# Windowed attention and a routed expert: the prologue rebuilt (batch 0's q and k in the weight buffers, V behind them, masks added by TensorE, pooling by tile, casts on three engines)

## The chip, the cores and the metric

One core of one Trainium2 chip. The time is device microseconds of one execution; the lower the better. "The kernel before" is the kernel as it was, "the changed kernel" the one with the change. A ratio is the mean time of one kernel's fast runs over that of the kernel before's fast runs of the same rounds, so it is not quite the ratio of the medians that are quoted. A run counts as slow when it is more than 1.5% above the fastest of the same kernel.

## The reference

```python
B, H, S, D = 8, 8, 576, 64          # attention, float32
scores = q @ k.T / 8
scores = where(abs(i - j) <= 32, scores, -1e9)
x = softmax(scores) @ v             # -> (8, 576, 512)
logits = x.mean(axis=1) @ w_gate    # one row a batch, 8 experts
e = argmax(logits)                  # one expert a batch
out = p[e] * (relu(x @ w1[e]) @ w2[e])     # w1 512x1024, w2 1024x512
```

What matters here: a batch's expert is known only after the attention of all its 576 rows, and only then can its two megabytes of weights be asked for. For seven of the eight batches another batch's work covers that. For the first there is nothing before it: that is the prologue. In what follows, the pooled sums are these column means, a bank is one of TensorE's output buffers, the mask is the window of the second line, and a semaphore is a counter by which a transfer tells that it has landed.

## The kernel before

A planner in the file orders operations by priority and by its own estimate of times, and emits them engine by engine. Batch 0's loads, all on SyncE's queue, V in two parts between q and k:

```python
buffers("raw", [P, 2, J, D], FP32, 5)          # q or k of half a batch
...
def load(op, b=b, quad=quad, name=name, src=src):
    t = op.got["raw"][0]
    nc.sync.dma_start(t..., src[b, 4 * quad : 4 * quad + 4]...)
plan.add("SP", 0.6, f"ld{name}{b}{quad}", load, takes=[("raw", 1)], land=650e3, prio=base + quad)
...
def msk(op, half=half, quad=quad):             # VectorE, every batch
    nc.vector.tensor_tensor(ev, ev, mv, ALU.mult)
...
def pool(op):                                  # 20 matmuls behind the last normalisation
    for dt in range(NDT):
        for i in range(NQT):
            nc.tensor.matmul(bank[:, dt : dt + 1], xs_of[(b, i)]..., onec, ...)
```

Each output tile is evacuated by ScalarE and its store issued by ScalarE at once:

```python
def evac(op, i=i):
    nc.scalar.activation(osb[:, 0:w], bank_of.pop(f"2{b}{i}")[:, 0:w], ACTF.Copy, ...)
...
def store(op, i=i):
    nc.scalar.dma_start(out[b, 128 * i : 128 * i + 128, :], osb)
```

The softmax here doesn't subtract the row's maximum and nothing guards it: scores larger than these inputs give would overflow.

## Time and profile before

| | kernel before |
|---|---|
| time | 241.48 us (241.28 to 241.85, 3 runs) |
| expert of batch 0 known | 29.68 us |
| its weights asked for | 32.70 us |
| first expert matmul | 42.20 us |
| pooled sums copied, batches 0 to 7 | 27.87, 51.29, 79.64, 105.20, 130.73, 156.27, 181.80, 207.35 us |

The last row is the clock of the whole kernel: from batch 2 to batch 7 one batch every 25.5 us. A shift that is made or lost anywhere shows as a shift of all later entries, and the interval in which it happened is the one that is not 25.5. The busy time by stretches shows the one place after the prologue where TensorE is not full (columns: stretch, then busy us of TensorE, its weight loads, VectorE, ScalarE and GpSimd, then granted clock, DMA share, GB/s):

```profile
60.00:80.00 20.00, 17.59 (x211) 14.23 (x209) 10.50 (x31) 10.46 (x23) 3.39 (x6) 0.91 1.02 303
```

and the waits of that stretch (us in total, times, longest) say that it is one wait of ScalarE:

```profile
ACT hT L775 <- issue: 4.5, 1, 4.5
...
PE bank L757 <- ACT hT L775: 2.4, 1, 2.4
```

"issue" there is the store that the prediction speaks of: ScalarE's queue stood at issuing it.

### The profile page before, as it was taken

The numbers are of one execution on the slowest core, as the hardware profiler recorded it, in microseconds if no ns is written. First come the engines' busy times: TensorE is split into PE (matmuls) and PEld (weight loads), VectorE is DVE, ScalarE is ACT, GpSimd is POOL, SyncE is SP. The second block draws the span as 40 slices with busy tenths as digits, with TensorE's granted clock in tenths as the row PEclk, the third lists the DMA queues.
The fourth block names the chain that finished last, engine by engine and source line by source line (L and its number), as shares of the span: only waits on it lengthen the run. The fifth ranks groups of instructions, "written<-read, shape, count | busy, mean of one in ns | idle before, by whom it ended". The sixth has DMA issues, their size and how long they took to land.

```text
span 240.9 us, 6498 instructions
## 1 busy us (share of the span) xinstructions
PE 222.2 (92%) x2602; PEld 178.4 (74%) x2602; DVE 152.4 (63%) x390; ACT 172.6 (72%) x345; POOL 88.3 (37%) x134
## 2 busy tenths in 40 slices
PE   7999897999969989998999899989999899999980
PEld 6887685997558956996599758975799569848740
DVE  7999869765743796668865896589667746300000
ACT  8698783669626796779767994799487967637640
POOL 7652583059022494019701890069203300110000
PEclk9999999999997999999999999999999999999996
DMA  6978999999999999989999999979912992099431
GB/s 232 270 211 253 327 298 226 260 386 208 244 328 325 322 242 210 339 275 290 195 325 312 268 213 288 300 191 216 251 33 24 190 229 106 3 166 228 154 135 61
DMA packets 30014, 55.02 MB, mean 228 GB/s; under 512 B 6560, under 2 KB 15648, under 8 KB 27936
## 3 DMA queue, kind: packets, MB, share of 16 engines
q0 software_dynamic: 2304, 16.78, 36.9%
q1 hardware_dynamic: 22032, 28.39, 35.7%
q10 hardware_dynamic: 5648, 9.44, 10.6%
q8 instruction: 20, 0.33, 0.5%
q14 instruction: 10, 0.08, 0.1%
HBM read 61.94 MB, written 9.44 MB: 296 GB/s over the span
## 4 chain that ended last, share of the span: by engine, by line
PE 57%; DMA 18%; ACT 8%; SPq 6%; DVE 5%; issue 2%; POOL 1%; ACTq 1%; POOLq 0%
PE bank L757 21%; PE bank L793 17%; DMA raw<-in_q_dram 8%; DMA w<-in_moe_w_dram 7%; PE bank L601 6%; ACT qT L372 5%; PE bank L639 3%; PE bank L522 3%; DMA raw<-in_k_dram 3%; DVE qT L370 2%; SPq L427 2%; PE bank L799 2%; ACT kT L372 2%; SPq L383 2%; PE bank L667 2%
## 5 line engine op out<-in xcount | busy, mean ns | idle before, releaser
L757 PE MATMUL bank<-xT,w 128*128 128x288 f16 x512 | 77.5, 291 | 3.9 <-ACT hT L775 2.4
L400 POOL CAST qkb<-raw 128x640 bf16<-128x640 f32 x64 | 52.5, 853 | 75.5 <-issue 36.7
L775 ACT ACTIVATE hT<-bank 128x288 f16<-128x288 f32 x128 | 52.0, 415 | 26.7 <-PE bank L757 15.1
L757 PEld LDWEIGHTS <-w 128*128 128x128 f16 x512 | 60.4, 146 | 4.8 <-issue 2.5
L793 PE MATMUL bank<-w,hT 128*128 128x512 f16 x256 | 60.5, 379 | 0.0
L819 ACT ACTIVATE osb<-bank,gwb 128x512 f32<-128x512 f32 (+1 forms) x40 | 26.3, 658 | 22.3 <-PE bank L793 18.0
L793 PEld LDWEIGHTS <-hT 128*128 128x128 f16 x256 | 23.8, 98 | 22.8
L554 ACT ACTIVATE E<-bank 128x512 f16<-128x512 f32 x72 | 40.4, 626 | 0.3 <-PE bank L522 0.3
L571 DVE TENSOR_TENSOR E<-E,mask 128x1024 f16<-128x1024 f16 (+1 forms) x40 | 31.1, 818 | 6.3 <-ACT E L554 6.0
L601 PEld LDWEIGHTS <-E 128*128 128x128 f16 x576 | 26.3, 99 | 5.8 <-issue 0.8
L601 PE MATMUL bank<-vaug,E 128*128 128x65 f16 x576 | 29.1, 195 | 0.6 <-DVE vaug L455 0.4
L522 PE MATMUL bank<-qT,kT 128*128 128x128 bf16 x288 | 24.5, 219 | 4.7 <-ACT qT L372 4.0
L522 PEld LDWEIGHTS <-kT 128*128 128x128 bf16 x288 | 19.9, 97 | 11.8 <-issue 5.2
L625 DVE TENSOR_TENSOR xs<-bank,linv 128x256 f16<-128x256 f32 x64 | 27.2, 425 | 2.2
L370 DVE COPY qT<-bank 64x640 bf16<-64x640 bf16 (+1 forms) x32 | 24.5, 772 | 5.5 <-ACT qT L372 3.0
L343 PE MATMUL bank<-wide,zero 128*128 128x256 f16 x170 | 26.0, 285 | 1.4 <-POOL wide L268 1.4
L623 DVE RECIPROCAL linv<-bank 128x4 f32<-128x4 f32 (+1 forms) x80 | 14.1, 176 | 20.7 <-PE bank L601 20.7
L372 ACT COPY qT<-bank 64x512 bf16<-64x512 bf16 (+1 forms) x32 | 23.5, 741 | 3.3 <-DVE qT L370 1.8
L475 PE MATMUL bank<-id_bf,qkb 128*128 128x128 bf16 x288 | 22.5, 219 | 1.5 <-POOL qkb L400 1.0
L440 POOL CAST vaug<-vraw 128x576 f16<-128x576 f32 (+1 forms) x32 | 22.5, 788 | 1.4 <-DMA vraw<-in_v_dram 1.4
L727 POOL DMA_DIRECT2D w<-in_moe_w_dram x8 | 4.7, 587 | 44.9 <-DVE gw L719 21.2
L475 PEld LDWEIGHTS <-qkb 128*128 128x128 bf16 x288 | 18.1, 98 | 2.8 <-POOL qkb L400 1.4
(63 smaller groups left out, 199.4 us busy)
## 6 DMA issues: line engine op xcount, KB each, us to landing
w<-in_moe_w_dram POOLq DMA_DIRECT2D x16, 1024.0 KB, 11.9
raw<-in_q_dram SPq DMA_DIRECT2D x16, 576.0 KB, 6.9
raw<-in_k_dram SPq DMA_DIRECT2D x16, 576.0 KB, 6.4
out_dram<-osb ACTq DMA_DIRECT2D x32, 256.0 KB, 5.8
out_dram<-osb ACTq DMA_DIRECT2D x8, 128.0 KB
vraw<-in_v_dram SPq DMA_DIRECT2D x1, 576.0 KB
vraw<-in_v_dram SPq DMA_DIRECT2D x1, 544.0 KB, 5.8
vraw<-in_v_dram SPq DMA_DIRECT2D x8, 8.0 KB
```

The source lines that it names most:

```text
L370: nc.vector.tensor_copy(dst, src)
L372: nc.scalar.copy(dst, src)
L400: nc.gpsimd.tensor_copy(dst, src)
L475: nc.tensor.transpose(pv[:, j - j0, :], qkb_of[(b, quad, name)][:, j], id_bf)
L522: nc.tensor.matmul(dst, qkT[(b, a, "k")][:, k0 : k0 + P], qkT[(b, a, "q")][:, :, k0 : k0 + 64], start=(m == 0), stop=True, skip_group_chec ...
L554: nc.scalar.activation(dst, src, ACTF.Exp, bias=0.0, scale=0.125)
L571: nc.vector.tensor_tensor(ev, ev, mv, ALU.mult)
L601: nc.tensor.matmul(bank[:, hp * 65 : hp * 65 + 65], E_of[b][:, h, c0 : c0 + P], va_of[b][:, late, slot, 0:65], start=(hp == 0 and n == 0), ...
L625: nc.vector.tensor_tensor(xv[:, quad], hv[:, :, 0:64], linv.to_broadcast([n, 4, 64]), ALU.mult)
L757: nc.tensor.matmul(bank[:, 0:288], w_of[b][0].rearrange("p t (c n) -> p t n c", c=P)[:, dt, ft], xT_of[b][:, dt, 288 * c : 288 * c + 288], ...
L775: nc.scalar.activation(h_of[(b, ft)][:, 288 * c : 288 * c + 288], bank_of.pop(gn)[:, 0:288], ACTF.Relu,)
L793: nc.tensor.matmul(bank, h_of[(b, ft)][:, 128 * i : 128 * i + 128], w2s[:, ft, :], start=(ft == 0), stop=(ft == NFT - 1),)
```

## The change

The intent: know batch 0's expert earlier, ask for its weights earlier, and so start the steady stage earlier. Its core, cut:

```diff
+    roomy = [t.rearrange(...).bitcast(FP32)... for t in (w1s[0], w2s[0], w1s[1], w2s[1])]
...
-                    t = op.got["raw"][0]
+                    t = op.got["raw"][0] if b else roomy.pop(0)
-                    nc.sync.dma_start(
+                    (nc.scalar if op.eng == "ACT" else nc.sync).dma_start(
...
+                other = b == 1 and quad == 0        # batch 1's first q, k: issued by ScalarE
+                plan.add("ACT" if other else "SP", 0.6, f"ld{name}{b}{quad}", load,
...
-                    plan.add("SW/ACT" if b == 1 else "SW",
+                    plan.add("ACT" if b == 0 and part else "SW/ACT" if b < 2 else "SW",
...
+                if b < EARLY:                       # EARLY = 2
+                    ... bias of 0 or -16384, one matmul a bank, before the scores
+                    nc.tensor.matmul(out, id_bf, bv, start=True, stop=True, skip_group_check=True)
...
-            if pp == 0 and half < 2:
+            if pp == 0 and half < 2 or b < EARLY:   # no mask on VectorE
                 continue
...
-        def pool(op):
+        for i in range(NQT):
+            def pool(op, i=i):                      # four matmuls a tile, as tiles come
```

V of batch 0 comes in one large transfer behind q and k; small constants move from VectorE to GpSimd. The diff also makes GpSimd's casts of batch 2 wait until batch 1's weights are asked for (a dependency named `W10_`), splits the matmul banks into two pools and changes the planner's own model of loads.

## The prediction

> **What bounds the kernel now.** I read the page first, then busy time by stretches, the chain of waits, and the timeline of the first 45 us.
>
> ```profile
> span 240.9 us, 6498 instructions
> PE 222.2 (92%) x2602; PEld 178.4 (74%) x2602; DVE 152.4 (63%) x390; ACT 172.6 (72%) x345; POOL 88.3 (37%) x134
> ...
> PEclk9999999999997999999999999999999999999996
> DMA  6978999999999999989999999979912992099431
> ```
>
> TensorE is the bound, but its 222 us are not all work. The row of the line that only multiplies zeros[...]:
>
> ```profile
> L343 PE MATMUL bank<-wide,zero x170: 271/273/418, 1.4 to 40.2; 128*128 128x256 f16 x170
> ```
>
> It runs until 40.2 us, so the kernel has a prologue of about 42 us (batch 0's attention, its routing, the load of the expert's first weights) and then a stage in which TensorE never runs dry:
>
> ```profile
> 40.00:50.00 10.00, 8.61 (x121) 8.09 (x120) 7.58 (x25) 5.16 (x13) 0.96 (x2) 1.00 1.02 282
> ...
> 80.00:100.00 20.00, 19.23 (x221) 14.56 (x219) 16.26 (x35) 16.19 (x32) 11.53 (x15) 1.00 1.01 269
> 100.00:120.00 20.00, 19.22 (x221) 14.97 (x220) 15.52 (x34) 16.97 (x35) 11.53 (x15) 1.00 0.98 264
> ```
>
> First column after the stretch is TensorE: 96% busy. The pooling matmuls recur at 78.96, 104.53, 130.06, 155.59 and 181.14 us, 25.5 us a batch. So a prologue shorter by x ends the kernel x earlier, if nothing gives it back before this pace sets in. The chain of waits shows what stands in that gap:
>
> ```profile
> 32.70 9.45 DMA w<-in_moe_w_dram
> ...
> 42.20 0.71 PE bank L757 x4
> ...
> 55.17 14.94 DMA raw<-in_q_dram
> 70.19 1.12 ACTq L832
> 71.36 0.42 ACT hT L775
> 71.82 1.18 PE bank L757 x8
> ```
>
> Batch 0's weights are asked for at 32.70, land at 42.15, and the first expert matmul follows. Later a q load of batch 3, issued at 55.17, lands at 70.11, and only then does ScalarE issue a store of batch 0 whose data was ready at 66.88 (its evacuation started at 66.41 and took 0.47): ScalarE stands for 4.5 us and TensorE for 2.4. The built program says why: the transfers of SP and ACT take eight completion semaphores in turn, and each waits for the one that used its semaphore before. The store shared one with that load.
>
> The prologue itself:
>
> ```profile
> 2.85 5.68 SPq L427 DMA_DIRECT2D vraw<-in_v_dram  x1
> ...
> 19.06 1.92 DVE L571 TENSOR_TENSOR E<-E,mask 128x1024 f16<-128x1024 f16 x3
> ...
> 26.40 0.42 DVE L625 TENSOR_TENSOR xl<-bank,linv 64x256 f16<-64x256 f32 x1
> ...
> 29.41 1.28 POOL L400 CAST qkb<-raw 128x640 bf16<-128x640 f32 x2 [0.15 <-POOL qkb L400]
> 29.53 0.15 DVE L701 FIND_INDEX8 idx<-top,lg 1x8 uint32<-1x8 f32 x1
> ...
> 32.70 0.69 POOL L727 DMA_DIRECT2D w<-in_moe_w_dram  x1 [0.37 <-issue]
> ```
>
> SP stands 5.7 us behind the first big V load, so the second k is issued at 8.58 and lands at 12.9; VectorE's last three mask multiplications (1.92 us from 19.06) run right up to its first normalisation at 20.91; the last normalisation ends at 26.8, the expert is known at 29.68, and GpSimd, still casting, asks for the weights 3.0 us later.
>
> [...] the q load above took 14.94 us beside two weight loads, against a median of 6.9. [...] In 56.0 to 62.8 us the weights (queue q0, big packets) starve the SP queue (q1):
>
> ```profile
> q0 software_dynamic: 157, 1.16, 84.0%
> q1 hardware_dynamic: 147, 0.22, 10.1%
> ```
>
> [...] here eight 512-column matmuls take 1.73 us in the chain, 216 each. [...] here the page's clock dips to 7 tenths just after the 2.4 us stall, with 288-column matmuls of up to 448 instead of 286 ns.
>
> **The change, part by part.** Batch 0's four q, k loads go into the idle weight buffers, back to back, V behind them. From the rates in the trace (first bytes at 2.2 us, some 0.38 MB/us for 2304-byte pieces) 2.36 MB land by about 8.5, so the second k comes 4.4 us earlier. V then shares the engines with batch 1's first q, k, now issued from ACT near 9.5; I expect it at 14 to 16, against 14.9: no gain, but none is needed.
>
> Masks: five VectorE multiplications leave batch 0 (0.69, 0.91 and 1.92 us) and five batch 1; TensorE gets 9 bias matmuls a batch, 9 x 0.216 = 1.9 us, in time that was filled with zeros (the order of the built program has 113 of those matmuls in place of 170). This costs nothing on the path.
>
> Casts: part goes to ScalarE, so in the new order VectorE makes eleven of batch 0's twelve transposed copies alone. It starts them at 7.75 (7.37 when its constants end before, plus an estimated 0.35 for the bias). Five of 0.72 to 0.83 for the first half, six more, 8.7 us in all with little waiting: 16.4. So the scores of the second half start at 16.6, as before (16.84). What shrinks comes after: four exponentials of 0.51 to 19.3, one gap copy 0.6, one V copy on ScalarE 1.15, to 21.1; then six normalisations at their pitch of 0.545: the last ends at 25.0, against 26.8.
>
> Pooling by tile leaves 4 of 20 matmuls behind the last normalisation (0.16 of 0.64 us), but a transpose ahead of them waits for a bank that ScalarE frees near 25.2; I put the expert's index at 27.9 (before 29.68). GpSimd has finished its casts by about 25.7 and asks 1.3 us later, the time it took for batch 1 (53.0 to 54.26): 29.2, against 32.70. Landing in 8.5 to 9.45 us: 37.7 to 38.6.
>
> ScalarE now becomes nearly equal to it: from 21.6 it has casts (2.0), ten transposed copies of 0.74, V casts (1.3), five copies of xT (2.6), the gate's exponential and eight or so exponentials of 0.51 before the third A·V tile that precedes the first expert matmul: about 38.4. So the expert stage starts at about 38.7, not 42.2: 3.5 us earlier.
>
> **What gives it back.** In the new program (its order of instructions, and which semaphore each transfer takes) the fourth store of batch 0 shares its semaphore with the first k load of batch 4, and that k waits for a buffer which GpSimd frees only after issuing batch 1's weights and six casts. Working: batch 1's weights are asked for 12.1 us after the stage starts (54.26 less 42.2), at 50.8, and their traffic lasts some 15.3 us (54.3 to about 69.6 before), to 66.1. By then 0.5 to 0.7 MB have passed beside them on SP's queue (before: 0.22 MB in 56 to 62.8 and 0.49 in 62.8 to 69.5); q and k of batch 4 are 1.18 MB, and some of batch 3's V may still be in front. The rest follows at 0.39 MB/us: the k lands at 67.5 to 69.5. The store is ready 23.7 us after the stage starts (65.88 less 42.2), near 62.4. TensorE runs on for GEMM2's last tile and two groups of batch 1, which come 24.3 us after the start and take 0.5 each: dry near 64.0, as the next bank is evacuated behind the store. It resumes one us after the landing, near 69.5: 5.5 us of stall, against 2.4. At that point one expert group, six A·V tiles and two transposes less are done than before (0.5 + 6 x 0.24 + 0.45 = 2.4 us). 69.5 + 2.4 = 71.9 against 71.8: the 3.5 us are gone, 241.6.
>
> **The rivals.** First: that store does not stand, because the load comes earlier or the weights let SP's queue through. Then 3.5 us are kept and the old stall with its half clock (2.4 + an estimated 1.7) goes too: 234 to 236. For it: nothing else is on the chain after 72; and the queue ran at 0.12 MB/us beside the first weights (0.77 MB in 42 to 48.5). Against: the order fixes that GpSimd frees the buffer after the weights are issued. Second: ScalarE is later than I count, the stage starts at 40, and the same stall moves with it: 243. Third: V's 256-byte pieces, still unfinished when batch 1's weights start, hold the k to 70.5 or later: 243 to 244. Fourth: V lands so late that batch 0's A·V waits for it (17 or more): the index slips by as much, about +1.
>
> **Range and chances.** I hold the give-back at about 77%, near 241.6, and the first rival at 23%, near 235.5; weighted 240.2, and I say 240.5. The range 235.8 to 243.8 takes most of both. Over 2% faster means under 236.65: only the first rival, 0.2. Over 2% slower means above 246.3: 0.04. Within: 0.76.
>
> **What would show it.** Right steps: no mask multiplications in the first 40 us; second-half scores near 16.6; index near 27.9; weights asked for near 29.2; first expert matmul near 38.7; then a store on ScalarE that waits until a k load lands near 68, and a TensorE gap of 5 to 6 us. Wrong: that gap missing or under 2 us (then 234 to 237); a first expert matmul after 40.5 or before 37; a batch pace other than 25.5.

## The result, and the profile after

The changed kernel: 250.28 us median (248.08 to 252.48, 4 runs) beside 241.66 (241.28 to 242.71) of the kernel before: ratio 1.0319, 95% interval 1.024 to 1.0398. It is slower, by more than the prediction's range allowed. The profiled run is the fastest of the four, 248.08 us; no other of the four was traced.

The page of the changed kernel. The clock row dips to 5 tenths where it dipped to 7, and the DMA row has a hole (0, 6) behind it, which was not there before: SyncE's next load waits 18.0 us, until 94.0, for a buffer that GpSimd's casts free, and these stand in GpSimd's queue behind batch 2's weights, asked for at 87.46 after the late pooled sums of batch 2.

```profile
span 246.4 us, 6422 instructions
...
PEclk9999999999959999999999999999999999999996
DMA  6999999999998069989999999979910994089431
```

The busy time by stretches shows where: TensorE has 14.17 of 20 us, 3.4 less than before, at a clock of 0.83.

```profile
60.00:80.00 20.00, 14.17 (x150) 10.89 (x149) 8.88 (x21) 7.88 (x18) 1.04 (x2) 0.83 0.96 303
```

The prologue, in the timeline (start, us, engine, line, operation, and in brackets the idle time before it and its releaser):

```profile
16.47 0.38 PE L564 MATMUL bank<-bias,id_bf 128*128 128x512 bf16 x1
...
25.96 0.42 DVE L675 TENSOR_TENSOR xl<-bank,linv 64x256 f16<-64x256 f32 x1
...
28.07 0.15 DVE L756 FIND_INDEX8 idx<-top,lg 1x8 uint32<-1x8 f32 x1
...
29.81 0.69 POOL L782 DMA_DIRECT2D w<-in_moe_w_dram  x1 [8.10 <-DVE gw L774]
...
39.76 0.71 PE L812 MATMUL bank<-xT,w 128*128 128x288 f16 x4 [1.65 <-DMA w<-in_moe_w_dram]
```

The expert is known at 28.22 instead of 29.68, the weights are asked for 2.9 us earlier, the first expert matmul comes 2.4 us earlier. So the prologue is faster in this trace. Then the chain of waits:

```profile
57.40 13.22 DMA raw<-in_k_dram
...
70.70 0.34 ACTq L885
...
71.09 0.48 ACT osb L874
...
71.61 4.17 PE bank L812 x20
```

The first k load of batch 4 lands at 70.62; only then does ScalarE issue the fourth store of batch 0, then evacuate the next bank, then TensorE goes on. The clock is halved for 6.83 us (68.01 to 74.84), where it was 3.41 us before (72.80 to 76.21), but not all of that is a loss. By stretches (columns as above), first the changed kernel, then the kernel before:

```profile
68.01:71.61 3.60, 0.00 (x0) 0.00 (x0) 0.00 (x0) 0.52 (x2) 0.00 (x0) 0.50 1.04 410
71.61:74.84 3.23, 3.23 (x14) 2.27 (x14) 0.00 (x0) 1.53 (x5) 0.00 (x0) 0.50 1.09 359
...
72.80:76.21 3.41, 3.41 (x34) 2.83 (x32) 1.22 (x4) 1.67 (x5) 1.28 (x2) 0.50 1.08 368
```

In 3.60 of the 6.83 us TensorE stands anyway; it works 3.23 us at half clock, against 3.41 before. So the half clock costs 1.6 us here and cost 1.7 before: it is part of what a stall costs, but not of the difference. In the list of waits:

```profile
ACT osb L874 <- DMA raw<-in_k_dram: 6.7, 1, 6.7
...
PE bank L812 <- ACT osb L874: 5.8, 1, 5.8
```

The pooled sums are copied at 26.80, 48.84, 84.84, 108.05, 133.56, 160.32, 187.02 and 212.55 us. Against the kernel before: 2.45 us ahead at batch 1, 2.85 behind at batch 3, 4.05 at batch 5, 5.22 at batch 6. So the stretch from batch 1 to batch 3 loses 5.3 us, and batches 5 and 6 lose 1.2 us each, which nobody had predicted. Of the 5.3, TensorE's idle time makes 4.05 (the stall 3.42 of it: 5.83 less 2.41), the half clock -0.1, and the rest, 1.3, is work: nine transposes more fall into this stretch (some 0.5 us at the 0.055 us from one to the next), and short gaps. There the timeline has, in the changed kernel,

```profile
141.52 4.46 POOL L425 CAST qkb<-raw 128x640 bf16<-128x640 f32 x7
...
141.74 4.78 DVE L618 TENSOR_TENSOR E<-E,mask 128x1024 f16<-128x1024 f16 x1
```

one mask multiplication of 4.78 us, as long as the run of GpSimd casts that started 0.2 us before it; and in the kernel before, at the same place of a batch,

```profile
137.65 6.79 POOL L400 CAST qkb<-raw 128x512 bf16<-128x512 f32 x7
...
139.72 3.12 DVE L571 TENSOR_TENSOR E<-E,mask 128x1024 f16<-128x1024 f16 x3
```

three masks in 3.12 us while seven casts take 6.79 instead of 4.46: there both engines go on, a cast taking 0.97 us instead of 0.64.

### The profile page after: what moved, and what is told of

It reads as the page before. It is cut to its first block, busy times and chain, and to the rows that moved or that the text cites.

```text
span 246.4 us, 6422 instructions
## 1 busy us (share of the span) xinstructions
PE 222.2 (90%) x2563; PEld 175.5 (71%) x2563; DVE 153.1 (62%) x375; ACT 174.8 (71%) x349; POOL 80.0 (32%) x136
## 4 chain that ended last, share of the span: by engine, by line
PE 44%; DVE 27%; DMA 13%; ACT 8%; issue 3%; POOL 1%; POOLq 1%; ACTq 0%; DVEq 0%
PE bank L812 19%; PE bank L848 9%; DMA w<-in_moe_w_dram 7%; PE bank L651 6%; DVE E L618 6%; DVE qT L393 6%; DMA raw<-in_k_dram 5%; ACT qT L395 5%; PE bank L689 4%; DVE vaug L491 3%; DVE kT L393 3%; DVE vaug L393 2%; PE bank L718 2%; DVE xs L675 2%; PE bank L569 1%
## 5 line engine op out<-in xcount | busy, mean ns | idle before, releaser
L812 PEld LDWEIGHTS <-w 128*128 128x128 f16 x512 | 61.0, 146 | 11.2 <-issue 7.8
L874 ACT ACTIVATE osb<-bank,gwb 128x512 f32<-128x512 f32 (+1 forms) x40 | 26.2, 656 | 26.7 <-PE bank L848 14.9
L425 POOL CAST qkb<-raw 128x512 bf16<-128x512 f32 (+1 forms) x53 | 38.5, 800 | 0.0
L618 DVE TENSOR_TENSOR E<-E,mask 128x1024 f16<-128x1024 f16 (+1 forms) x30 | 29.6, 1029 | 4.7 <-ACT E L601 4.4
L651 PE MATMUL bank<-vaug,E 128*128 128x65 f16 x576 | 27.5, 193 | 1.8 <-DVE vaug L491 1.0
L569 PEld LDWEIGHTS <-kT 128*128 128x128 bf16 x288 | 20.5, 97 | 11.6 <-issue 3.5
L651 PEld LDWEIGHTS <-E 128*128 128x128 f16 x576 | 24.5, 97 | 5.1 <-DVE vaug L491 1.4
L393 DVE COPY qT<-bank 64x640 bf16<-64x640 bf16 (+1 forms) x33 | 25.3, 775 | 3.0 <-ACT qT L395 2.2
L569 PE MATMUL bank<-qT,kT 128*128 128x128 bf16 x288 | 25.2, 219 | 2.2 <-ACT qT L395 1.9
L364 PE MATMUL bank<-wide,zero 128*128 128x256 f16 x113 | 17.8, 303 | 1.4 <-POOL wide L285 1.4
L469 POOL CAST vaug<-vraw 128x576 f16<-128x576 f32 (+1 forms) x26 | 18.3, 790 | 0.0
## 6 DMA issues: line engine op xcount, KB each, us to landing
raw<-in_k_dram SPq DMA_DIRECT2D x13, 576.0 KB, 15.3
```

What stands on the lines that cost most here:

```text
L393: nc.vector.tensor_copy(dst, src)
L425: nc.gpsimd.tensor_copy(dst, src)
L569: nc.tensor.matmul(dst, qkT[(b, a, "k")][:, k0 : k0 + P], qkT[(b, a, "q")][:, :, k0 : k0 + 64], start=(m == 0 and b >= EARLY), stop=True, ...
L651: nc.tensor.matmul(bank[:, hp * 65 : hp * 65 + 65], E_of[b][:, h, c0 : c0 + P], va_of[b][:, late, slot, 0:65], start=(hp == 0 and n == 0), ...
L812: nc.tensor.matmul(bank[:, 0:288], w_of[b][0].rearrange("p t (c n) -> p t n c", c=P)[:, dt, ft], xT_of[b][:, dt, 288 * c : 288 * c + 288], ...
```

## The experiments

Theory A: a store that ScalarE must issue stands until the load that used its semaphore before has landed, and this (the wait, and the half clock behind it) is most of the loss. Rivals: GpSimd's runs of casts shut VectorE out and that is the loss (theory P); or the prologue is not faster at all in most runs. Which semaphore a transfer takes is fixed when the program is built; of the changed kernel (its packed trace agrees: the transfers of SyncE and ScalarE take eight numbers in turn, 101 and 104 to 110, GpSimd's weight loads eight others, 112 to 119, and the k load issued at 57.40 and the store issued at 70.70 both have 106):

```
k load of batch 4, first half   semaphore 3   after V of batch 2
...
store 4 of batch 0              semaphore 3   after k load of batch 4, first half
store 5 of batch 0              semaphore 4   after store 1 of batch 0
```

| run | median us (range) | kernel before | ratio (95%) |
|---|---|---|---|
| e1 two stores to SyncE | 243.08 (240.10 to 244.78) | 240.51 | 1.008 (0.9986 to 1.0173) |
| e2 kernel before, one store to SyncE | 244.16 (243.98 to 245.18) | 240.51 | 1.0177 (1.0115 to 1.0239) |
| e3 casts wait for a copy | 253.36 (250.78 to 257.20) | 240.51 | 1.0477 (1.0388 to 1.0565) |
| e4 e1 and e3 | 247.11 (244.64 to 247.73) | 240.51 | 1.0263 (1.0173 to 1.0352) |
| e6 e1, casts wait for the masks | 242.05 (239.91 to 244.46) | 240.89 | 1.0012 (0.9938 to 1.0086) |
| e7 e6 and two prologue edits | 241.48 (240.14 to 243.38) | 240.89 | 1.0029 (0.9955 to 1.0102) |
| e8 e1, masks back on VectorE | 244.03 (241.64 to 245.24) | 240.89 | 1.0138 (1.0058 to 1.0218) |
| e9 changed kernel again | 250.42 (249.68 to 252.58) | 240.89 | 1.0376 (1.0295 to 1.0457) |
| e10 e7, third store to SyncE | 239.11 (238.13 to 240.26) | 242.06 | 0.9897 (0.9854 to 0.9939) |
| e11 e7, third store to GpSimd | 239.93 (239.03 to 240.85) | 242.06 | 0.9931 (0.9889 to 0.9973) |
| e12 e6, third store to GpSimd | 237.99 (237.02 to 239.68) | 242.06 | 0.9842 (0.9794 to 0.989) |
| e13 kernel before, one store to GpSimd | 241.54 (239.86 to 246.00) | 242.06 | 0.9984 (0.994 to 1.0028) |
| e14 e12, loads held for the weights | 245.66 (243.77 to 249.36) | 241.67 | 1.0165 (1.0114 to 1.0217) |
| e15 e12, 16 zero matmuls | 237.62 (237.05 to 238.10) | 241.67 | 0.9841 (0.9797 to 0.9885) |
| e16 changed kernel, three stores moved | 240.58 (238.57 to 242.62) | 241.67 | 0.9939 (0.9883 to 0.9994) |
| e17 e12 again | 240.73 (237.70 to 242.81) | 241.67 | 0.9926 (0.9862 to 0.9991) |
| e18 kernel before, three stores moved | 244.08 (242.43 to 245.68) | 242.15 | 1.0105 (1.0045 to 1.0165) |
| e19 e15 again | 238.53 (237.00 to 240.00) | 242.15 | 0.9858 (0.9802 to 0.9915) |

All gave the reference's result. Calls were e1 to e4, e6 to e9, e10 to e13, e14 to e17, e18 and e19; only runs of one call share a chip and rounds, so compare across calls by ratio. In the edits i counts a batch's stores from 0.

### The waiting store: e1, e9, e2

e1, on the changed kernel:

```diff
+                by = nc.sync if b == 0 and i > 2 else nc.scalar
-                    nc.scalar.dma_start(out[b, 128 * i : 128 * i + 128, :], osb)
+                    by.dma_start(out[b, 128 * i : 128 * i + 128, :], osb)
```

> The changed kernel with one edit: the last two stores of batch 0 are issued by SyncE instead of ScalarE, ahead of the q and k loads of batch 4, so that no store of batch 0 waits for a load in flight. Theory A (the store's wait for the k load of batch 4 emptied TensorE and halved its clock): ScalarE's evacuation at about 70 us no longer waits 6.7 us, the half-clock stretch near 71 to 75 us goes, the pooling of batch 3 comes 5 us earlier, and the time is 245 us or less (242 to 245 if VectorE's two long waits of the late batches stay, 238 to 241 if they go as well). Rival B (the long VectorE waits behind GpSimd's casts, or a prologue that was never faster, made the loss): the stall goes but the time stays at 247 to 251 us. Rival C: the q and k loads of batch 4, now issued at 62 to 63 us instead of 54 to 57, land too late for batch 4's transposes and the stall comes back near 85 to 95 us; time 247 us or more with TensorE waiting on a transpose.

Measured: ratio 1.008. Its own stretch, which is the one to hold against the two above (the profiled run, 244.78 us, was the one slow run of its four):

```profile
60.00:80.00 20.00, 20.00 (x228) 15.66 (x226) 15.76 (x32) 15.51 (x33) 5.29 (x9) 1.00 1.00 283
```

TensorE is full and the clock is whole: the stall is gone, and rival C (q and k of batch 4 too late) did not come about. e9, the changed kernel unedited:

> The changed kernel once more, unedited, for the spread of its prologue and its stall beside the others on the same chip. If the store's wait for the k load of batch 4 is in every run: ScalarE again waits 5 to 7 us near 64 to 70 us, with half clock behind it, and the time is 248 to 252.5 us; the index at 27.4 to 30 us; VectorE's long waits in batches 5 and 6 again. If the stall was an accident of the first trace: 243 to 246 us.

Measured 250.42 us; the stall is again there and longer (TensorE waits 7.36 us, until 76.39). So the wait is in the kernel, not in one run, and two stores moved are worth 1.0319 or 1.0376 against 1.008: 2.4 to 3.0%, 6 to 7 us, most of the loss. The traces say the same: from batch 1 to batch 3 the changed kernel took 59.21 us and e1 51.65, 7.6 us less, of which the wait is 5.8 and the half clock behind it 1.6. Theory A holds for most of the loss. It is not all: e1's trace again has batches 5 and 6 1.2 us late (26.74 and 26.70 us).

e2 asked what the old stall was worth in the kernel before:

```diff
+                by = nc.sync if b == 0 and i > 3 else nc.scalar     # the fifth store of batch 0
```

> The kernel before with one edit: the fifth store of batch 0 (the one that waited for a q load of batch 3 in flight) is issued by SyncE. Theory A: that wait cost 2.4 us of TensorE plus the half clock that followed it (3.4 us at half clock, some 1.7 us of work), so the time falls from 241.6 to about 237.5 us (237 to 239). Rival B (TensorE makes up such a stall from its backlog, so it costs nothing): 241 to 242 us, unchanged.

Measured 244.16 us: 1.2 to 2.4% slower than without the edit. Both expectations missed the time, but not the place: the pooled sum of batch 2 came at 74.45 instead of 79.64, 5.2 us earlier, of which 1.0 was there at batch 1 already: 4.15 us, the 2.4 of the wait and the 1.7 of its half clock. Then the chain shows the next one:

```profile
77.39 19.89 DMA out_dram<-osb
...
97.36 1.12 ACTq L833
...
98.53 0.42 ACT hT L775
...
98.99 2.08 PE bank L757 x8
```

The moved store was issued by SyncE only at 77.39, behind a V load, and took 19.89 us beside two weight loads; the fifth store of batch 1 uses its semaphore next, and ScalarE stood until 97.3. TensorE waited 5.1 us. The mechanism of theory A again, with a store in the load's place.

### The casts: e3, e4, e6

e3 (and e4, the same edit on top of e1) makes GpSimd wait for VectorE's first row-moving copy:

```diff
+    if b > 3 and quad == part == 0 and name == "q":
+        nc.gpsimd.tensor_copy(junk, va_of[b - 1][0:1, 1, 0, 0:1])
     nc.gpsimd.tensor_copy(dst, src)
```

> The changed kernel with one edit: before its q and k casts of batches 4 to 7 GpSimd reads one element of what VectorE's first row-moving copy of the batch before wrote, so it waits for it; the casts then start when VectorE is already inside its run of copies and masks. Theory P (an unbroken run of GpSimd casts keeps a waiting VectorE instruction out for the whole run, 4.78 us and 3.81 us in the changed kernel's trace, and the pooling of batches 5 and 6 slips by 1.2 us each): no VectorE mask or copy is longer than 1.5 us, the casts alternate with it (about 0.97 us each instead of 0.64), time about 2.4 us less: 246.5 to 248.5 us, and the spread between runs shrinks. Rival (VectorE's wait is off the path that sets the end): time as the changed kernel's, 249 to 251 us, with the long instructions gone all the same. The stall at 70 us stays in both.

> Both edits together on the changed kernel: the stores of batch 0 moved to SyncE, and the casts of batches 4 to 7 held until VectorE's first row-moving copy. If the two losses are separate and together are all of it, the gain of the prologue of 2.4 us and the 4.1 us of the stall that the kernel before has too are left: 236 to 239 us, faster than the kernel before by 1 to 2 per cent. If the prologue gives nothing in the end: 240 to 242. If a third cause is at work: above 243.

Measured 253.36 and 247.11 us: not the gain that was expected, and rather a loss (e4 against e1: 1.0263 against 1.008, intervals that just touch; e3 has no unedited changed kernel in its call, and its interval overlaps those of the others, 1.0319 and 1.0376). The timeline of e4 shows why:

```profile
89.09 0.47 POOL L427 COPY junk<-vaug 1x1 f16<-1x1 f16 x1 [0.37 <-DVE vaug L494]
89.50 4.94 POOL L428 CAST qkb<-raw 128x640 bf16<-128x640 f32 x8
...
89.54 5.21 DVE L494 COPY vaug<-vaug 64x1152 f16<-64x1152 f16 x1
```

VectorE was in its run of copies and its next copy took 5.21 us all the same, until the eight casts beside it (89.50 to 94.44) had ended; its other copies take 0.46. The expectation that the casts would alternate with a VectorE that is already at work did not hold here. e6 holds the casts until the masks are done instead:

```diff
+    if b > 3 and b - 1 in screened:      # set where the last mask of a batch is emitted
+        screened.remove(b - 1)
+        nc.gpsimd.tensor_copy(junk, E_of[b - 1][0:1, 0, 8 * P : 8 * P + 1])
```

> The kernel with the two stores moved to SyncE, and one more edit: GpSimd's q and k casts of batches 4 to 7 (six or eight of each batch's eight) wait for VectorE's last mask of the batch before, instead of its first copy. Holding them for the first copy made it worse (247 against 243 us): the casts took the next VectorE copy's place for 5.2 us, twice. Theory P (VectorE shut out by an unbroken run of casts delays the masks, and TensorE waits for the masks: 1.2 us in each of batches 5 and 6): no VectorE instruction over 2 us in the late batches, the pooling of every batch from 3 on comes 25.5 to 25.7 us after the one before, and the time is 2 to 2.5 us under the 243 us of the moved stores alone: 240 to 241. Rival (the order matters[...]: the interval stays at 26.7 us in batches 5 and 6): 243 us or more.

Measured 242.05 us, ratio 1.0012. No VectorE instruction of the late batches was over 2 us any more, and batch 6 came 25.87 us after batch 5. But batch 5 still came 26.69 us after batch 4, and the chain there names a wait of the first kind: a store of batch 3 behind a q load of batch 7 that was issued at 134.87 and took 14.21 us. So the held casts free VectorE, but that load went out only when one of them had ended (134.16 and 0.69 us), and behind its landing TensorE waited 1.16 us.

### The third store: e7, then e10, e11, e12, e16, e17

e7 added two edits in the prologue to e6. Two traces of the same prologue, e3's (index at 27.40) and e1's (index at 29.89), differ first here, e3 then e1:

```profile
10.55 0.44 PE L514 MATMUL bank<-id_bf,qkb 128*128 128x128 bf16 x5 [0.89 <-DVE qT L394]
...
12.90 0.38 PE L567 MATMUL bank<-bias,id_bf 128*128 128x512 bf16 x1
...
18.38 0.74 DVE L494 COPY vaug<-vaug 64x1152 f16<-64x1152 f16 x1
```

```profile
10.70 0.44 PE L511 MATMUL bank<-id_bf,qkb 128*128 128x128 bf16 x5 [2.08 <-DVE qT L393]
...
14.09 0.63 PE L564 MATMUL bank<-bias,id_bf 128*128 128x512 bf16 x1
...
19.64 1.97 DVE L491 COPY vaug<-vaug 64x1152 f16<-64x1152 f16 x1
```

In e1 the twenty zero matmuls from 3.65 us on took 2.83 us against 3.86 in e3, so TensorE came through its queue a microsecond earlier, ran out of zero matmuls and idled 2.08 us; the clock halved (a 512-column matmul takes 0.63 instead of 0.38), and then a copy took 1.97 us while GpSimd's casts of batch 1 ran (17.99 to 21.29).

```diff
+    for _ in range(10 if first and b == quad == 0 and name == "k" else 0):
+        warm(op)                                   # ten zero matmuls
...
+    if b == 1 and not held:                        # casts of batch 1 wait for the first copy
+        nc.gpsimd.tensor_copy(junk, va_of[0][0:1, 1, 0, 0:1])
```

> The same kernel with two more edits in the prologue: ten zero matmuls more ahead of the first k transposes, and GpSimd's casts of batch 1 wait for VectorE's first row-moving copy of batch 0. In two of the four traces of the new prologue TensorE ran at half clock from 11 to 15 us after 2 us of idling, and that copy took 1.97 us instead of 0.74: the index came at 29.9 us instead of 27.4 to 28.1. Theory S (these two random costs are what hides the prologue's gain): no half clock before 40 us, the copy takes under 0.9 us, the index at 27.5 to 28.5 us, the first expert matmul at 39 to 40.5, the spread between runs narrows, and the median is 1 to 2.5 us under that of the kernel without these edits: 238 to 239.5, faster than the kernel before by about 1 per cent. Rival (the weights' landing is bound by transfers, not by when they are asked for): the index is early, the first expert matmul still at 42 us, time unchanged.

Measured 241.48 us. The prologue did as expected (copy 0.46 us, index at 27.44, first expert matmul at 39.65, no half clock before 40), and batch 4 was pooled at 124.98, 5.75 us ahead of the kernel before. And then batch 5 came 29.17 us later:

```profile
130.59 15.11 DMA raw<-in_q_dram
...
145.78 0.54 ACTq L900
...
146.36 0.42 ACT hT L842
...
146.83 0.65 PE bank L824 x4
```

The fifth store of batch 3 and the first q load of batch 7. This is the third place where a store waits for its predecessor's semaphore. e10 issues that store from SyncE, e11 from GpSimd, e12 is e11 without the two prologue edits:

```diff
-                by = nc.sync if b == 0 and i > 2 else nc.scalar
+                by = nc.sync if b == 0 and i > 2 else nc.gpsimd if b == 3 and i > 3 else nc.scalar
```

> The kernel with moved stores, held casts and the two prologue edits, and one more: the fifth store of batch 3 issued by SyncE, for in that kernel's trace it is the one that waits for a load in flight (the q load of batch 7, issued at 130.59 us, 15.1 us to landing; TensorE dry 2.06 us and half clock behind it, the pooling of batch 5 29.17 us after that of batch 4, where 25.55 is usual). Theory A (any store of ScalarE whose semaphore is held by a load in flight stops TensorE): batch 5 comes 25.6 us after batch 4 and the time falls by 3 us or so, to 237 to 239 us, 1 per cent or more under the kernel before. Rival: the next of such waits takes its place (the last q and k loads of batch 7 are now issued behind that store), 240 to 242 us.

> The same, with that store issued by GpSimd, whose transfers have semaphores of their own, so that SyncE's loads stay where they were. Theory A: as with SyncE, 237 to 239 us, and no wait of the loads behind the store. Rival: GpSimd's issue of the store holds up its casts of batch 7 and TensorE waits for the transposes near 155 to 160 us: 240 or more.

> That without the two prologue edits (ten more zero matmuls; casts of batch 1 held for VectorE's copy), which tells what these are worth once no store waits. If the prologue's random costs matter: 1 to 2.5 us above the run with them and a wider spread, 238.5 to 241. If they are made up later: the same within 0.5 us.

Measured 239.11, 239.93 and 237.99 us: all below the kernel before, and in all three traces batch 5 comes 25.4 us after batch 4. The prologue edits gain nothing here: with them the ratio is 0.9931, without them 0.9842. Their mechanism was seen in the trace, their worth was not; why the kernel with them is if anything slower stays open, for the two traces are alike (first expert matmul at 40.46 and 40.51, last pooled copy at 204.09 in both).

e16 leaves out the held casts, e17 repeats e12:

> The changed kernel with its three waiting stores moved (two of batch 0 to SyncE, one of batch 3 to GpSimd) and nothing else, to size GpSimd's runs of casts without the stalls. Theory P: batches 5 and 6 again come 26.7 us after the one before, and the time is 2 to 2.5 us over the version with held casts in this call: 240 to 240.5 us. Rival (the held casts gained nothing by themselves): 238 us, as that version.

> The version with the three stores moved and the casts held, once more beside the others on one chip: 237 to 239.7 us, 1 to 2 per cent under the kernel before, as in its first call. If that was luck of the chip: within 1 per cent of the kernel before.

Measured 240.58 and 240.73 us, ratios 0.9939 and 0.9926. This is the plainest test of theory A: moving three stores and nothing else takes the changed kernel from 1.0319 and 1.0376 to 0.9939, so the whole loss, and not only most of it, goes when these stores are moved (compared by ratio, for the calls were on different chips; the third move also breaks a run of casts, as said below). Theory P falls as a cause of the time: with the casts held, batch 6 comes 25.88 us after batch 5 in place of 26.70, 0.8 us in the trace, and no difference in the times that these runs resolve. (Batch 5 is not late in e16 either, 25.36 us: GpSimd stands 7.7 us at the moved store, which breaks the run of casts.) That e6 was better than e1 may be this or luck between calls. And e17 was partly a miss: 0.7%, not 1 to 2.

### The prologue's gain: e8, e14, e15

Nine traces have the new prologue up to the weights' landing unedited, four have the old. Means, and the range in brackets:

| us | old prologue (4) | new prologue (9) |
|---|---|---|
| index search starts | 29.39 (29.15 to 29.53) | 28.60 (27.40 to 29.94) |
| weights asked for | 31.92 (31.43 to 32.70) | 30.34 (29.13 to 31.67) |
| from there to the first expert matmul | 9.50 (8.81 to 9.94) | 10.74 (9.95 to 11.29) |
| first expert matmul | 41.42 (40.70 to 42.20) | 41.08 (39.76 to 42.84) |
| half clock right behind it | 1 of 4 | 8 of 9 |

The request is 1.6 us earlier, the expert stage 0.3: the weights take 1.2 us longer. (Two of the traces are of slow runs, e1 and e13; without them the stage is 0.5 us earlier, 40.86 against 41.35.) The trace of the changed kernel (39.76) was the luckiest of nine. e8 undoes one part, on e1:

```diff
-EARLY = 2
+EARLY = 0
```

> The kernel with the stores moved, and the part that adds the masks of batches 0 and 1 by TensorE undone: VectorE multiplies them in again. The prediction put the last normalisation of batch 0 at 25.0 us and counted five masks of about 0.8 us off VectorE's way in the prologue. If that part carries the prologue's gain: the index comes 2 to 4 us later than with it (30 to 33 us) and the time rises by 2 us or more. If the loads and casts carry it: the index within 1 us of the 28 to 30 us seen, and the time within 1 us of 243.

Measured 244.03 us. The index search starts at 32.42, 2.5 us later than in e1: the masks on TensorE are the part that carries the earlier index, as predicted. (It is 3.8 us later than the mean of the nine, and 3.0 later than the old prologue: what else the change does to the prologue had made the index later.) But the first expert matmul comes at 43.54 against 42.84, 0.7 us later: most of it is given back in the weights' flight (9.4 against 11.2 us). e1's trace was the slowest of the nine, though; against their mean the stage is 2.5 us later and 1.3 are given back. The time does not size the masks: the interval overlaps that of e1, and in e8 too a store waited, the fifth of batch 1 behind a q load of 19.96 us, and TensorE with it for 2.62 us. e14 asks what they fly beside, on e12:

```diff
+                if b == 2 and half == 0:           # ahead of V of batch 2, on SyncE
+                    nc.sync.dma_start(hold, w_of[0][0][0:1, 0, 0:2])
```

> The best version so far (stores moved, casts held for the masks; 237.99 us) with one edit: ahead of V of batch 2, SyncE copies one element of the first weights, so V of batch 2 and the q and k loads of batch 3 aren't sent before these weights have landed. In the new prologue 10.8 MB of other data move before the first weights' last packet, in the old 9.7 MB, and the weights take 9.95 to 11.3 us from request to the first expert matmul where the old ones took 9.5 to 9.9. Theory T (the earlier request is given back because the new order puts V of batch 2 ahead of the weights): from request to first expert matmul 9 us or less, first expert matmul at 38 to 39 us instead of 40.5, no half clock there, time 1 to 3 us less: 235 to 237. Rival (the weights' own megabyte and its descriptors take that long): 10.5 to 11 us as without the hold, time unchanged or worse, for batches 2 and 3 then wait for their data.

Measured 245.66 us, and both theories are half right. In its profile (a slow run, 249.36 us, used for distances and for the order of events, not for the time) the weights are asked for at 32.60 and used at 41.43:

```profile
32.60 0.69 POOL L792 DMA_DIRECT2D w<-in_moe_w_dram  x1 [11.43 <-DVE sexp L783]
...
41.43 0.71 PE L822 MATMUL bank<-xT,w 128*128 128x288 f16 x4
```

8.83 us, the shortest of any new prologue, and no bracket: TensorE was not kept waiting. The request itself was late in this trace, which could shorten the flight by itself; the bytes on the other queues between the request and the landing tell more. They were 0.02 MB here for 8.8 us, 0.4 for 8.8 (e18), 0.7 for 9.3 (e8), 1.1 for 9.4 (the kernel before) and 1.2 to 1.7 for 9.9 to 11.2 in the nine. So the loads that the new order sends ahead of the weights do take back what the early request gains. But held back they come later, and a store waits for one of them, TensorE with it for 8.4 us:

```profile
77.70 24.63 DMA raw<-in_q_dram
...
102.40 1.13 ACTq L898
...
104.04 1.12 PE bank L822 x4
```

e15 treats the other half of the loss, the half clock, on e12:

```diff
+                    for _ in range(16 if b == ft == c == 0 else 0):
+                        warm(op)                   # ahead of the first expert matmul
```

> The best version with sixteen zero matmuls (0.11 us each) ahead of the first expert matmul, in the time in which TensorE waits 2.6 us for the weights. In seven of nine traces of the new prologue 3.4 us at half clock begin there, where TensorE idled 2.1 to 2.9 us; where it idled 1.65 and 1.78 us there was none. Theory H (the half clock takes back 1.7 us of what an early arrival gains): no half clock before 60 us and 1 to 1.7 us less time: 236.3 to 237.3. Rival (the lost 1.7 us is made up in the backlog of batch 1): unchanged, 237.5 to 238.5.

Measured 237.62 us (237.05 to 238.10, the narrowest spread of the experiments), ratio 0.9841 against 0.9926 of e17: 0.85%, 2.0 us; the intervals just overlap. But e12, which is e17, had 0.9842 without these matmuls. It was run at another time. (The expectation left out e10, where TensorE idled 2.41 us and the clock was not halved.) The clock row and the first expert matmuls of e12's first trace, then of e15:

```profile
PEclk9999998899999999999999999999999999999997
...
40.51 1.18 PE L819 MATMUL bank<-xT,w 128*128 128x288 f16 x4 [2.60 <-DMA w<-in_moe_w_dram]
```

```profile
PEclk9999999999999999999999999999999999999996
...
39.88 0.71 PE L821 MATMUL bank<-xT,w 128*128 128x288 f16 x4 [1.32 <-DMA w<-in_moe_w_dram]
```

Four matmuls in 1.18 us become 0.71, and there is no half clock until the kernel's end. e19 ran it once more, beside a kernel before with its three waiting stores moved (e18):

```diff
+                by = nc.gpsimd if b == 0 and i > 3 or b == 1 and i > 2 else nc.scalar   # e18
```

> The version with the three stores moved, the casts held and sixteen zero matmuls before the first expert matmul, again, beside the stall-free kernel before: 237 to 238.2 us, within 0.5 us from run to run, 1.5 per cent under the kernel before. If the new prologue is worth anything once no store waits in either kernel: 0.5 to 2 us under the other of this call; if not, the same.

> The kernel before with the three stores moved to GpSimd that waited in its own traces and in those of its edits: the fifth of batch 0, the fourth and fifth of batch 1. With the fifth of batch 0 alone the next wait came in batch 1 (a k load of batch 4 and a q load of batch 4 held the two stores' semaphores; TensorE dry 2.5 us at 97 us). Theory A (the old prologue would be nearly as good if no store waited): 237 to 239 us, 1.3 to 2 per cent under the kernel before, within 1 per cent of the changed kernel without stalls. Rival 1 (the waits move on a third time): 240 to 243 us with TensorE dry at another place. Rival 2 (GpSimd's casts come late behind the stores): TensorE waits on transposes near 105 us, 240 or more.

Measured 238.53 us (0.9858) and 244.08 us. e15's version is 1.4 to 1.6% under the kernel before, and here under e18 as well; but it spread from 237.00 to 240.00, so the narrow spread of e15 did not come again. e18 missed: up to batch 3, pooled at 99.52, it is 5.7 us ahead of the kernel before and level with e15 (99.64) and e19 (101.22); then batch 4 comes 31.2 us later, behind a store of batch 2:

```profile
103.33 17.95 DMA raw<-in_q_dram
...
121.35 1.13 ACTq L833
...
122.99 1.12 PE bank L757 x4
```

e13 was the same attempt with one store moved:

> The kernel before with one edit: the fifth store of batch 0 issued by GpSimd. Issued by SyncE it took the old stall away (the pooling of batch 2 came at 74.45 us instead of 79.64) but got in the way of the fifth store of batch 1, which uses its semaphore next and waited for it until 97.28 us. Theory A: without either wait the kernel before takes 4 us less, about 237 us; then the whole change, with its own stalls removed, gains only 0 to 1 us over it. Rival: another store comes to wait in its turn: 240 to 244.

Measured 241.54 us: the rival. Its profile (a slow run) has the next wait at the two stores of batch 1 that e18 then moved. What the whole change is worth with no waiting store in either kernel is therefore open; one trace, at batch 3, says about nothing.

## Why the prediction was wrong, point by point

Its mechanism was right: the store, the load, the semaphore, the resumption one microsecond after the landing. Its answer, "71.9 against 71.8: the 3.5 us are gone, 241.6", failed at three steps: the landing of batch 0's weights, the landing of the k load of batch 4, and "nothing else is on the chain after 72".

- **Index at 27.9, weights asked for at 29.2, start of the expert stage at 38.7.** In the first trace 28.22, 29.81 and 39.76; over nine traces the search starts at 28.60, the request is at 30.34 and the stage starts at 41.08. The term that was mis-sized is "Landing in 8.5 to 9.45 us": 9.95 to 11.3. The prediction took the flight of the old prologue; the new one sends more data ahead of the weights (e14: 8.83 us without them). The cost of the masks was right in direction (e8: 2.5 us of index).
- **Second-half scores at 16.6, last normalisation ends at 25.0.** 16.47, and 26.38. The sum as written, 21.1 and six times 0.545, comes to 24.4; the other 0.6 is not accounted for. The bias, put at 0.35, took 0.24 us. The count ran over ScalarE; in the trace the ten normalisations follow one another from 19.90 on, behind an A·V that waited for VectorE's row-moving copy (18.61 to 19.35), which the count did not hold. In e1's trace they start at 22.16 (half clock at 11 us, a copy of 1.97 us).
- **k of batch 4 lands at 67.5 to 69.5, TensorE dry at 64.0, a stall of 5.5 us.** 70.62, 65.78 and 5.83 us: the load 2.1 us later than the middle of that span and TensorE dry 1.8 us later, of which the stage's late start is 1.06 in both. The other 1 us of the load: batch 1's weights moved for 15.7 us in place of 15.3, and the term that was mis-sized most is "The rest follows at 0.39 MB/us": in 66 to 70 us SyncE's queue moved 0.98 MB, 0.25 MB/us, while 0.62 MB of stores passed on ScalarE's queue. The stall's size was right to 0.3 us, because both its ends came late.
- **The half clock was not missing.** The prediction gave it 1.7 us in a rival's sum and no difference in its own, and that came out: 1.6 us of work lost behind the stall, against 1.7 before. Later traces have a half clock at the stage's start too (8 of 9), another 1.7 us, which e15 took away. In e9's trace (252.58 us) it is there, in the first (248.08) it is not; that it makes the median 250 is likely, but the median's runs were not traced.
- **"Nothing else is on the chain after 72".** Batches 5 and 6 lost 1.2 us each. In those places a VectorE instruction lasts until a run of GpSimd casts has ended (4.78 us from 141.74, the run to 145.98; 3.81 from 169.08, the run to 172.58); holding the casts brought batch 6 back to 25.9 us, but not a time that the runs resolve.
- Together, in the first trace's span: TensorE goes on at 71.61 instead of 69.5, 2.1 us late (1.06 of it the stage's start); short gaps between batches 1 and 3, outside the stall, make 0.6 more than before; batches 5 and 6 make 2.4. These are 5.1 of the 5.5 us by which it is longer than before (246.4 against 240.9), where the prediction had none. Two of its own signs of being wrong came: a batch pace other than 25.5 (26.7, twice), and, in six of the nine traces though not in the first, a first expert matmul after 40.5.
- **The rivals.** "That store does not stand": it stood in both traces of the changed kernel. Taken away by hand (e1) the kernel did not fall to 234 to 236 but to 243, because the kept gain of the prologue was 0.3 and not 3.5 us, and in its trace there are a half clock at the stage's start and the late batches 5 and 6. "ScalarE is later" named the start that the first trace had (40; 39.76), but there TensorE waited 1.65 us for the weights and not for ScalarE. "V's 256-byte pieces" named the landing (70.5 or later; 70.62) and the nearest time, 243 to 244, short by 6; but the last of V, in pieces of 1024 bytes, had gone by 54 us. The chance of 4% for slower was far too low: the range covered the terms that were listed, each with its own spread, and nothing for a term that was not.

What stays open: why a VectorE instruction sometimes lasts until a run of casts has ended and sometimes does not; why the two prologue edits of e7 gained nothing; what the change is worth without any wait; and what the dependency `W10_` does, without which the k load of batch 4 might have been sent earlier.

## What to carry to other kernels

In a program that issues its stores from a computing engine, list for every store which transfer used its semaphore before, and when that one can land: here stores of batches 0, 1, 2 and 3 stopped TensorE for 1 to 8 us that way in one version or another, and each time one was moved the next in line had to be looked up. When a bound engine is made to wait, add the clock that it loses afterwards (1.7 us behind a wait of 2.41 us in the kernel before, 1.6 behind 5.83 in the changed kernel, none behind 2.62 in e8: not in proportion to the wait), but count only the half-clock time in which it works; a few zero matmuls in front of an awaited instruction removed such a loss. And an earlier request is not an earlier landing when the same change also sends other data first.

## What the traces show of the hardware

- Half clock came here after last gaps of 1.64 (e13), 1.94 (e17), 2.00 (e16) and 2.60 us (e12), and did not come after 2.41 us (e10): the length alone does not tell. The stretch at half clock at the stall was 3.41 us long in the kernel before and 6.83 us in the changed kernel.
- With no cast beside it a row-moving copy of VectorE takes 0.46 us and a mask 0.56 (changed kernel, 146.54 to 150.69). Beside a run of GpSimd casts one such instruction took 3.8 to 5.2 us, until the run had ended, in some places (a mask 4.78 and a copy 3.81 us in the changed kernel, a copy 5.21 in e4); in others both went on (three masks in 3.12 us, 0.97 us a cast instead of 0.64, kernel before).
- Where transfers of several issuers use completion semaphores in turn, ScalarE stood 6.7 us at issuing a store whose data was ready (changed kernel), until the k load that had the same semaphore had landed.
- With 1.2 to 1.7 MB on the other queues between the request and the landing, against 0.4 to 1.2 in the old prologue, the weights' way from request to use grew from 9.5 to 10.7 us in the mean.
